# The first batch of a fused attention and feed-forward kernel, worked in two parts of its tokens

## The chip, the core and the metric

The kernel runs on one core of one Trainium2 chip. The metric is device microseconds (us) of one execution, lower is better. All times are of the same inputs, drawn with a fixed seed.

## The reference

Two stages. The first is attention that keeps only the scores within `tau` of the row's maximum; the second takes the largest of three products and multiplies it out again.

```python
q, k, v: (8, 8, 576, 64)        # batch, heads, tokens, head size; float32
scores = q @ k.T / 8
scores = where(scores >= max(scores) - tau, scores, -1e9)     # tau = 0.02, by row
attn = exp(scores - max(scores)); attn = attn / (sum(attn) + 1e-9)
x = (attn @ v), heads side by side: (4608, 512)
h = maximum(maximum(x @ w1, x @ w2), x @ w3)                  # w: (512, 768)
out = h @ w_out                                               # (4608, 512), float32
```

## The kernel before

**Tiling.** The 64 heads are worked in 16 groups of four ("quads", two to a batch). A quad's scores come in nine chunks of 128 rows, each chunk of two "halves" of 128 x 576 (`r` is 0 or 1): 288 halves in all, in the order of the list `steps`. Eight of the nine chunks belong to one half of the quad's head pairs each, the fifth is shared; chunks 0, 1, 5 and 6 hold the first 256 tokens of the batch.

**What each letter does.** The order of all work is written out by hand in the table `ORDER`, one letter for each step, in which a digit names one of four PSUM slots (`bank`, 128 x 1024 floats, two banks each). The wrapper `_Ordered` makes every engine run its instructions in exactly that order. A score half passes through these steps:

- `S` (TensorE): `scores`, into a slot. `m` (VectorE): `maximum`, the row maximum, which also leaves a copy of the scores in a buffer z. `s` (VectorE): `threshold`, a tiny step that some halves need.
- `e` (ScalarE): `exponents`, a first pass over the half. `n` (ScalarE) or `k` (VectorE): `numerators`, the second pass with the row sum. Which of the two is decided by a digit in the table `MASKED`: for 1 and 3 the second pass is on VectorE (`masked`), for 0 and 2 on ScalarE, and then a `0` needs the threshold. For 2 and 3 the first pass reads the slot itself, otherwise z (`direct`).
- `r` (VectorE): the reciprocals of a chunk. `p` (GpSimd): one half of the weights P in bfloat16. `t`: an SP-issued DMA that transposes the chunk's P into `ptq`.

`T` transposes q or k of a quad on TensorE, `a` and `c` copy it out (ScalarE and VectorE), `q` copies q with the partition halves swapped (GpSimd). `O` is a product of `ptq` with v, copied into `xt` by `w` (VectorE) or `x` (ScalarE). `F` and `B` are the two halves of a feed-forward piece. A hidden piece (`hid`) computes 128 columns of one of the three x @ w for all 576 tokens, in two runs of 288 tokens, one to each bank of its slot; its contraction is cut in two halves of 64 rows that run side by side in the array ("row-tiled", `halves`), and `B` swaps the two. The first of the three is copied to a buffer `hm` by ScalarE (`h`), the second is maximised into `hm` and the third into `hT` by VectorE (`v`, `v`). An output piece (`outp`) makes two chunks of 128 rows of the result, copied by `u` and stored by `o`. `N` makes the rows that are left over. `l` issues a load of q, k or v, `g` a load of a block of weights through a double buffer `stage`, `z` casts it on GpSimd, `y` casts v.

**The parts.** `SPLIT` names batches whose tokens are worked in two parts, chunks 0 and 1 first (256 tokens) and then chunks 2 to 4 (320 tokens): the scores, products and feed-forward pieces of the first part come before those of the second. Before, this is the last batch alone (batch 7), so that the program's end does not wait for all of its scores. There a hidden piece has a single run, on all 128 rows of the array, and an output piece is one chunk.

Of the kernel before, what the change touches and what calls it, by code (L numbers as in the profile page):

```python
# [21 lines left out]
FLAT = 2.0 ** -100  # L22

MASKED = """
232222322322222222021032222202332122123122200200111000000000100000000011
000010111020011000101000000001100001001000010011111100000000100100000000
110010030111000100010000000001010100001110001011010100110000000000000000
100101101011000000120000001010000000110011100000001110001000010011111021
"""


# [10 lines left out]
gS0pmelT2mqnS3tcpemqS2nlkT1eytaS0rmnT1kpermS3yS2enczrmS1qT0enmepnqtS3nprmaymgpeS0lptS2mppT0mtpS1enencnqsS3re  # L42
rmtpS0mS1penmS3lqnsS2mtperpekzllmT0tmpenkT1pgS3eearnS0petmnqrS2meqlnpS3lmnplsS2cetpremS1pS0nmplermtzeS3mnS2p
mtnpmS3rkpS1leektS0emnrpmemptS1eekS2pO3mktS0rennmpermT2pnS1wptemS3prkyO0tmeakS2pgS1enxlnrmS0lpesS2mezT3mS1np
mgntspcS2eqrseT3mtpeS0srmapS1mnT2ptS3mnqO0ceqmeO1prswnptnkS3pxS0meF1meS2zBresmT0qghF3klpF2nkBtaS1sveS0pemF3B
nyrrsmyBepT1svS0hpcT2nS3zmaS1erpgsF2mntpsBmnS3yvF1etssT0myeBprS2cnpS3mnS0ympelF2epF3lmBnzslssvS0htBrqmeS2vpn
S1gF0sepmF3teqBmF2erssvpBtnBkphF0eS1vtS3znmF2nrBmqteS1rpvBnS3pmlnF0pmgeS1qsBsrhmS3pevS2npS1mF0npsO3ermpesmO2
zewepgsskBxtT3nF1vS2nklBarS0mlphS3mtepF2sS1rmnyBmetF3pvT0eBpcnS2tzT1nvS0asmzS3temS2qeS1meF0trkpmS3lenpBmnlys
reklpF1umerpskS3upBeoketmS0uS2umpS3tesmS1qeT0myO2nqlrsnlprcO3etqsmepwS0xptS1mnF3psnmS2BlerskpS1thF0meF3pmeBF
2ktnBveBsrS1nvpS0hmyF3emF2npBrssT0eprtvBaF1kS3nqvBeF0myhyS2kyleF3mBelBvnpS2snsS0vptemS1pnF3rmpT2tnBmpeF0scS1  # L50
htBrnmpF3erT2rpvlBasS1pstvnS2pmeF0pS3emtBqnmT2S1hcqS3empF2eS0rsqmtS1epsmBeF3pmnF0stsvBeBknF2klhF1BvelS0nrvpB
emT3pS2arvS0ptnS3mpnO1smtesrkpeF2swnlrpmeT0S1qtescS3epBmnpmnT0trskS3paS1umS0ulqmeS3lmyS1nopS2smelS0rmeS3psmn
O1ypersmqO2etkpemO0lewqxlknpS3tS1keF2momS3lexF0ktT1enkBercpnsBpumN1ertkphkF3jS0rursS1empBnmF2ptS0vpS1smeF3yt
BsnsmBpnvS0pT1hmF2atT3srepS0cF1eprBsmeqF3vnByBynvplS2nsS0plmhS1mteS2mF0nF3mteS1rrspBnmS2pelvBlepF1smT0leqBvl
# [50 lines left out]
def kernel(  # L105
# [31 lines left out]
    NF = DF // 128  # L137
# [341 lines left out]
    def ffn(b, part):  # L479
# [46 lines left out]
        def outp(cs):  # L526
# [16 lines left out]
                my["h"][0]()  # L543

            def done(a):
                if a == 0 and (part is None or c % 2 == 0):
                    st["ob"] = hp_.tile([128, 2, DM], F32, name="ob")
                both = st["ob"]
                ob = both[:, a if part is None else c % 2]
# [6 lines left out]
                if part is not None:  # L556
# [36 lines left out]
        def ninth():  # L593
# [10 lines left out]
            def done():  # L604
# [225 lines left out]
```

## Time and profile before

| | |
|---|---|
| timed runs (3), median | 446.8 us (446.54 to 447.92) |
| the profiled execution: span | 444.8 us |
| TensorE matmul busy | 422.4 us, 95% |
| ScalarE busy | 403.0 us, 91% |
| VectorE busy | 392.8 us, 88% |
| GpSimd busy | 311.9 us, 70% |
| the chain that ended last | 86% TensorE, 5% ScalarE, 4% VectorE |

No time of the profiled execution is given beside its span; the median of the timed runs is 2.0 us above that span. In the profile PE is TensorE, PEld its weight loads, DVE VectorE, ACT ScalarE, POOL GpSimd, SP the engine that issues most DMAs. Nearly every instruction has the line of the helper `run` (L93 before, L95 after), so groups are told apart by the names of what they write and read: sc are scores, tp transposed q and k, o the products, ph hidden pieces, po output pieces, z the score halves on their way (`stage` too, which lends its buffers to them later on).

### The profile page before, as it was taken

How to read it: one execution, taken by the hardware profiler on the slowest of the kernel's cores; microseconds unless marked ns; L12 is line 12 of the kernel's file. 1: busy time of each engine (PE TensorE's matmuls, PEld its weight loads, DVE VectorE, ACT ScalarE, POOL GpSimd, SP SyncE). 2: the span in 40 equal slices, each digit the busy share in tenths (PEclk: the TensorE clock that was granted, in tenths of full speed). 3: DMA queues.
4: the chain of work that ended last, by engine and by line, in shares of the span. 5: the costliest groups of instructions: out<-in, count | busy, mean ns of one | idle time of the engine just before them, and what ended most of it. 6: DMA issues, size and time to landing. Idle time of an engine off the chain costs nothing.

```text
span 444.8 us, 14254 instructions
## 1 busy us (share of the span) xinstructions
PE 422.4 (95%) x5188; PEld 320.2 (72%) x5190; DVE 392.8 (88%) x1228; ACT 403.0 (91%) x836; POOL 311.9 (70%) x420
## 2 busy tenths in 40 slices
PE   7767789999999999999999999999999999999996
PEld 6334347787788767787788777788688886787873
DVE  3887999999999999999999999998999998899642
ACT  3999999999999999999999999899999999987632
POOL 2799989997878687696785877676676685457400
PEclk8998999999999999999999999999999999999999
DMA  7999999999999999699899999989999977487633
GB/s 188 275 293 199 291 169 269 235 243 262 229 180 194 212 222 292 125 256 167 143 234 189 230 198 203 209 168 210 208 206 194 244 151 105 83 179 136 145 116 108
DMA packets 213959, 88.50 MB, mean 199 GB/s; under 512 B 189184, under 2 KB 202240, under 8 KB 213888
## 3 DMA queue, kind: packets, MB, share of 16 engines
q1 hardware_dynamic: 213360, 86.96, 95.9%
q8 instruction: 41, 0.67, 0.6%
q10 hardware_dynamic: 528, 0.62, 0.5%
q14 instruction: 30, 0.25, 0.2%
HBM read 35.65 MB, written 9.44 MB: 101 GB/s over the span
## 4 chain that ended last, share of the span: by engine, by line
PE 86%; ACT 5%; DVE 4%; issue 2%; DMA 1%; SPq 0%; DVEq 0%; ACTq 0%
PE ph L93 32%; PE sc L93 32%; PE po L93 10%; PE o L93 9%; ACT z L93 5%; PE tp L93 3%; DVE z L93 3%; DMA qm<-in_q_dram 1%; ACT qt L93 1%; SPq L93 0%; DVE xt L93 0%; DVE hm L93 0%; DVE stage L93 0%; DVE rs L93 0%; ACT ob L93 0%
## 5 line engine op out<-in xcount | busy, mean ns | idle before, releaser
L93 POOL TENSOR_SCALAR P<-z,rs 128x576 bf16<-128x576 f32 x250 | 200.6, 814 | 63.3 <-DVE rs L93 28.1
L93 DVE TENSOR_SCALAR_CACHE_REDUCE z<-sc 128x576 f32<-128x576 f32 x250 | 183.7, 750 | 14.8 <-PE sc L93 10.1
L93 PE MATMUL sc<-kt,qs 64*128 64x256 f32 (+2 forms) x640 | 182.6, 423 | 5.7 <-DVE z L93 2.3
L93 PE MATMUL sc<-kt,qt 64*128 64x320 f32 (+2 forms) x640 | 182.4, 433 | 5.2 <-ACT z L93 3.3
L93 PE MATMUL ph<-xt,w 64*128 64x288 bf16 (+2 forms) x2160 | 170.8, 283 | 0.1
L93 PEld LDWEIGHTS <-w 64*128 64x128 bf16 (+1 forms) x2160 | 130.1, 94 | 28.6 <-issue 4.3
L93 ACT ACTIVATE z<-z 128x576 f32<-128x576 f32 x174 | 117.6, 679 | 0.1
L93 PEld LDWEIGHTS sc<-kt,qs 64*128 64x128 f32 (+1 forms) x640 | 92.4, 180 | 25.7 <-DVE z L93 5.7
L93 ACT ACTIVATE z<-z,th 128x576 f32<-128x576 f32 x143 | 106.2, 769 | 5.0 <-DVE th L93 4.2
L93 PEld LDWEIGHTS sc<-kt,qt 64*128 64x128 f32 (+1 forms) x640 | 91.9, 179 | 19.7 <-ACT z L93 5.9
L93 DVE SCALAR_TENSOR_TENSOR z<-z 128x576 f32<-128x576 f32 x76 | 62.2, 830 | 0.5 <-ACT z L93 0.5
L93 PE MATMUL po<-wo,hT 64*128 64x512 bf16 (+3 forms) x454 | 53.5, 354 | 0.3
L93 POOL COPY qs<-qt 64x640 f32<-64x640 f32 (+3 forms) x66 | 43.0, 652 | 10.8 <-ACT qt L93 7.2
L93 ACT ACTIVATE z<-z,nm 128x576 f32<-128x576 f32 x68 | 50.6, 767 | 0.0
L93 DVE TENSOR_TENSOR hm<-ph,hm 128x576 bf16<-128x576 f32 (+2 forms) x54 | 37.0, 686 | 9.2 <-PE ph L93 8.9
L93 ACT ACTIVATE hm<-ph 128x576 bf16<-128x576 f32 (+2 forms) x54 | 31.8, 589 | 13.4 <-PE ph L93 12.8
L93 POOL TENSOR_SCALAR P<-stage,rs 128x576 bf16<-128x576 f32 x38 | 30.4, 804 | 19.3 <-ACT z L93 5.4
L93 PEld LDWEIGHTS <-hT 64*128 64x128 bf16 (+2 forms) x456 | 30.0, 95 | 16.5 <-issue 2.3
L93 DVE TENSOR_TENSOR hT<-ph,hm 128x576 bf16<-128x576 f32 (+2 forms) x54 | 37.0, 686 | 4.0 <-PE ph L93 2.3
L93 PE MATMUL o<-ptq,vb 128*64 128x64 bf16 (+2 forms) x544 | 39.0, 281 | 0.0
L93 ACT ACTIVATION_READ_ACCUMULATOR z<-z 128x1 f32 x174 | 34.3, 197 | 0.0
L93 PEld LDWEIGHTS <-vb 128*64 128x64 bf16 x544 | 23.3, 111 | 12.8 <-issue 4.9
(45 smaller groups left out, 431.6 us busy)
## 6 DMA issues: line engine op xcount, KB each, us to landing
vm<-in_v_dram SPq DMA_DIRECT2D x32, 256.0 KB, 4.8
qm<-in_q_dram SPq DMA_DIRECT2D x15, 512.0 KB, 5.0
km<-in_k_dram SPq DMA_DIRECT2D x15, 512.0 KB, 5.3
out_dram<-ob SPq DMA_DIRECT2D x14, 512.0 KB, 4.0
stage<-in_moe_w_dram SPq DMA_DIRECT2D x9, 512.0 KB, 5.2
ptq<-P SPq DMA_TRANSPOSE x144, 4.0
vr<-in_v_dram SPq DMA_DIRECT2D x16, 128.0 KB, 3.4
stage<-in_moe_w_out_dram SPq DMA_DIRECT2D x3, 512.0 KB, 4.9
```

Source lines behind the costliest of these rows:

```text
L93: ins = fn(*a, **kw)
```

## The change

- Batch 0 is put into `SPLIT` too, with the same two parts as batch 7, and into a new set `PAIRED`.
- In a paired batch a hidden piece holds two groups of 128 hidden columns (2f and 2f+1) of one part's tokens, one group to each bank of its slot, instead of one group with two runs of tokens. So it stays row-tiled with two halves `F` and `B`; there are 9 such pieces a part, 18 in the batch as before. Their maxima are kept in `hT` from the first of the three on, with no `hm`.
- Its output pieces are (0, 1) and (2, 3) instead of (0, 2) and (1, 3), one after each part.
- `ORDER` and `MASKED` are written anew. `ORDER` has four `O` more (40 for 36, with two `w` and two `x` more), since batch 0 has eight half-sized products for four. In `MASKED`, 95 halves have their second pass on VectorE (86 before) and 27 their first pass from the slot (41 before).

```diff
-SPLIT = {7: ((0, 1), (2, 3, 4))}
+SPLIT = {0: ((0, 1), (2, 3, 4)), 7: ((0, 1), (2, 3, 4))}
+
+PAIRED = {0}
...
-llllllglllT0laclT1laclzllqqS0qqS1meS2mS3lmlT0enlkS1ylmlT2eamelrnpS3leqlmnyS1qcapS0emtnrcS3pmnT2qmepgrelS1qya
+lllllllllT3lcalqqT1S0lacqqlmS3lemlkegT0lS2calnT1qS3lycamlmqelqreqS2gynpS0nmlpS1ezmreS2lpmpeT0mgyaknT1qT3cT0a
...
-        gap = 2
-        chunks = ([(0, 2), (1, 3)] if part is None else [(c,) for c in mine]) + ([4] if part is None or 4 in part else [])
+        paired = part is not None and b in PAIRED
+        gap = 1 if paired else 2
+        chunks = ([(0, 2), (1, 3)] if part is None else [tuple(mine)] if paired else [(c,) for c in mine]) + \
+            ([4] if part is None or 4 in part else [])
...
-        nr, n = len(runs), runs[0][1] - runs[0][0]
+        nr, n = 2 if paired else len(runs), runs[0][1] - runs[0][0]
...
-                c0, c1 = runs[a]
+                c0, c1 = runs[0 if paired else a]
+                k = 2 * f + a if paired else f
                 return (my["ps"][:, a * 512:a * 512 + n],
-                        lambda rows: wts[wi][rows, kc, f * 128:(f + 1) * 128],
+                        lambda rows: wts[wi][rows, kc, k * 128:(k + 1) * 128],
...
-                    st["hm", f] = hp_.tile([128, nr, n], BF16, name="hm", bufs=3)
+                    st["hm", f] = h_of(b)[:, 2 * f:2 * f + 2, S * (b % 2) + runs[0][0]:S * (b % 2) + runs[0][1]] if paired else hp_.tile([128, nr, n], BF16, name="hm", bufs=3)
...
-                    dst = hm if wi == 1 else \
+                    dst = hm if wi == 1 or paired else \
...
+                if paired:
+                    if a == 1:
+                        stores.append(lambda: sync.dma_start(
+                            out=rows_out[:, 0:8].rearrange("p (x c s) m -> p x s c m", x=2, c=2)[:, :, c // 2], in_=both))
...
-        return ([hid(f, wi) for f in range(NF) for wi in range(3)],
+        return ([hid(f, wi) for f in range(NF // 2 if paired else NF) for wi in range(3)],
...
-                later = [outs.pop()] if part is not None and part != parts_of(b)[-1] else []
+                later = [outs.pop()] if part is not None and b not in PAIRED and part != parts_of(b)[-1] else []
```

Three places in the order. The first is TensorE after its first scores: here stand the transpositions (tp) of the second quad's q and k. Before, they are spread among the scores of the first quad:

```order
131 L93 MATMUL tp<-identf,qm 128x64 x8
132 L93 MATMUL tp<-identf,q_147 128x64 x2
133 L93 MATMUL sc<-kt,qt 64x320 x2
134 L93 MATMUL sc<-kt,qs 64x256 x2
135 L93 MATMUL sc<-kt,qs 128x256
136 L93 MATMUL sc<-kt,qt 128x320
137 L93 MATMUL tp<-identf,km 128x64 x8
138 L93 MATMUL tp<-identf,k_149 128x64 x2
```

After, all four stand together, behind the eighth score half, and the next score is the second quad's:

```order
127 L95 MATMUL sc<-kt,qs 128x320
128 L95 MATMUL sc<-kt,qt 128x256
129 L95 MATMUL tp<-identf,qm 128x64 x8
130 L95 MATMUL tp<-identf,q_147 128x64 x2
131 L95 MATMUL tp<-identf,km 128x64 x8
132 L95 MATMUL tp<-identf,k_149 128x64 x2
133 L95 MATMUL tp<-identf,qm 128x64 x8
134 L95 MATMUL tp<-identf,km 128x64 x8
135 L95 MATMUL sc<-kt,qs 128x256
```

The first quad has eighteen score halves; before, all of them came first.

The second place is SP's queue around the eighth transposed chunk. Before (rows 23, 25 twice, 28 three times and 30 are the second to the eighth; `stage` is a load of weights):

```order
25 L93 DMA_TRANSPOSE ptq<-P 128x9x128 x2
26 L93 DMA stage<-in_moe_w_dram 128x4x256
27 L93 DMA vr<-in_v_dram 64x8x64
28 L93 DMA_TRANSPOSE ptq<-P 128x9x128 x3
29 L93 DMA vr<-in_v_dram 64x8x64
30 L93 DMA_TRANSPOSE ptq<-P 128x9x128
```

After (row 33 is the eighth):

```order
26 L95 DMA stage<-in_moe_w_dram 128x4x256
27 L95 DMA_TRANSPOSE ptq<-P 128x9x128
28 L95 DMA vm<-in_v_dram 64x4x256 x2
29 L95 DMA_TRANSPOSE ptq<-P 128x9x128
30 L95 DMA stage<-in_moe_w_dram 128x4x256
31 L95 DMA_TRANSPOSE ptq<-P 128x9x128
32 L95 DMA stage<-in_moe_w_dram 128x4x256
33 L95 DMA_TRANSPOSE ptq<-P 128x9x128
```

Ahead of the eighth stand seven weight loads after the change, four before.

The third place is VectorE at its first feed-forward maximum, which stands behind 55 row maxima before:

```order
92 L93 SCALAR_TENSOR_TENSOR z,sm<-z 128x576 x2
93 L93 TENSOR_SCALAR th<-nm 128x1
94 L93 TENSOR_TENSOR hm<-ph,hm 128x576
95 L93 TENSOR_SCALAR z,nm<-sc 128x576
96 L93 RECIPROCAL rs<-sm 128x2 x2
```

and behind 34 after, two in a row and of two groups of 256 tokens each:

```order
70 L95 TENSOR_SCALAR th<-nm 128x1
71 L95 RECIPROCAL rs<-sm 128x2
72 L95 TENSOR_TENSOR hT<-ph,hT 128x2x256 x2
73 L95 TENSOR_SCALAR z,nm<-sc 128x576 x2
74 L95 COPY kt<-tp 128x2x256
```

So the first batch's pieces have moved forward past some twenty score halves.

More of the change, by code (lines that the diff above doesn't have):

```diff
@@ L24 @@
 MASKED = """
[L25 to L28, printed above, removed]
+122222122222220303001010100100100000301001203001300200001230000001301020
+000110100001001010100010000100110001011100011100101010000000100010010100
+000100102011110010100010000001001010000011111001101100000100000000000101
+000011110100110000001100000010000000101111000110020110001000110011201003
 """
@@ L45 @@
[L45 to L54, printed above, removed]
@@ new lines @@
+pnS3lmeprsmntpmeS2gpseT0mS1znkS2etyS3esrgkpnmapmO1etzT0wnS2lrmepT1cO3agpsnrmS0lpxsS1lemqO3lekO2pnswrmxS3zeS0
+tmeF1pkF2ngqF3esBmBnqkBhF0qesrsBrvteS1pvS2nlpmF3hzmeT1BcnptS0ssngvF1pS2mepBretmS3zeF2mpnrsvS3pnBtmepS1gepS0s
+rmT3hzmteS1skpF0agmnBS2pevO3tkeyS0rnwmeS3pmnO2ytmpnT1lszxF3celBrskepS1evS2trznmT3S0ntsmpF1alkpelrmS2elpBmeqn
+sktS2eplO3muupS0srwnS2pmeO1mqeT3ktpS2xnrsF1cnT0mqtS3aqrsBlmeyT0phS2sctnS3pmF0eprS1metpBsmnF3pveS2tyBremS0pet
+vynpmF3ekS1qntS0smeT2ByrkapS1nsmlS2hprlmF0epS3mnBtqssmeF1lpvT2elS3psrncBpmeS0tS2psnvlO3nmqleqmO1erwpleskF2px
@@ new lines @@
+S0kntS3mnS1rmBepS0mepS3trmhpnsmS2pteF0srmpeS3skytT2nS1maBrmntyS2pveF3peS1smpBnsmS0tynrvS2pleT1mpS3ectqT0nmF1
+eymtnsrklS2eplsT3amBeylkqelcS0nsrS2spmuO3umqekpS2ewtS0nS1prmnS3pmO2essyrmepmS0elpS1smxS3pnsmtF2qeF0mlBnlrkBp
+hS3srevF2tpeS1mlpS0nmBpnF3myS1evBetkF0elF2mhBorkpS1nssF3vetBysmpeBlrS0evpS1hsmpT2eF3meF0tkBakBnqF2tvnS1srvpn
+S3trmBeplS0smhpS1oempT2lF3nmyS0ncBteF1srmpS2evT0qBmaF3pnlrsvS0peS2smS1pntmBeF0rmphS2keBqF1nmtT3qevBF2pesrvlS
+0epclT1nBpsmS3aktF0nkF1hBsrmepBrveO2ptevpnS3swqS1tnmF2pnrkpteS3meS0pmS1tnrmBpesmpeS0tkuT3essrO1cputekS3yxmoS
@@ new lines @@
+2nmlpT0eS1mqeS3mO2nktaO1rnkpewS0epmS2xsyrsmF3pekyetS1meqS0mnlqBmnlpskleT0N1rucpluskpS2jS3nmtF0erS1rmpeS2mpBm
+F3phS1ssekptT2nBmlT0arvlpS1ecF2lpS3nmqS0estmF1eBomBnvS3htrkS0pnF2lssssemF1yBemBntvyS3pervS0peF2srmpF1emBptnB
+kphF0sreS3vS2pnmBpeF1vnT3qBmaS0slhS2meS3srnS1mtpF0nmpF2esBrmpF3esvpBetBvqF0hkqS1tnS2meBrmT3epO1vnplceT0kF2at
+S3sswnqBmeT0O1rvnpcetqF2xklS0pnrsS1lmnS3ymeBptS0shsyrmS1eF2rmpetF3mBpeS0vpnBsmpteT1S2vpaS0nmtS1nsrmF2pnmtpes
+S3kyeS1mByermpelskS3nqS0emO1tpemlnqrS0wupS3meF1tpkenO0kuktnT2rmlpxBceplrsrS0kpluS3usmoF2eymS1eS0ismpBeS3mpht
@@ new lines @@
+S1nmpF0emS2S3nsrssmpBnF1pveT2trBmaF0veqS3tkeByF1hkF2temBplnS0ssvpoBemlS3erlrS1vpnF0mnqF2tsmeBpBkhF1ynrS3svpn
+S0mtBperS2vepF3mnpT1BmptS0hspF2nmT3BcaS0elsqvS3S1nmF2tersrpmF0nBmpBevqT3hS1scpteF2mplT0nS3klS1asmBeqO0mtesnk
+O1erwpevF3ptxS0skyeS2srF1mnBmetpBvlS0phS2srnmqF1nmT3pF0erctBypeBsvT3yS2pvaS1nmpS3temS0qlnmF2emtnS3rkpleS1rml
+S0epBmepsmpT1uO3cetkelO1kulnkF0yxwosrkepS1teS2mpnS3mBeyrsmpeS2kpuS3tumN1nlmqeorkS2pjlS3emlF1pssT0meS2ketF3rB
+armpBhkpF0nF1trvnBqsBvS3phrsF0tempS1espS2mS3nqBsmetF1pmnF2pvBnS3psevBteysrF0mpF1hkpBntF2ervT3pBncBpvS0hrS3se
@@ new lines @@
+pmT2epS1maS0slmF3nmF2nBsteBrsvpS1eipvT0nF3smqeS2tBmS1lhcF2nsS3mtnBsrspeS0vS1pemO2nqmtemT3lnS0wS1amF2etF3rsmp
+eBspS0nvS1eqmBnF2rkpF0htsmBeS3pveS1rmeO2pmnptknByS3xvS1nrmT2tpS0ssmepS3meyF1cnemS0teS2rmplBnkyermO3pusklepO2
+ulwepkT3xS1akS0leT2smF3nrcptesmS1poeS2rmpeF0lkBeqmnBkqtuS2usslS1hmqS3lnrmpF0eF2kyBesmF1etBrrvpnS3ospBnvF0mhp
+S2etspBmnF3prvS1epBnmT0tpvS2aS1smeqtT3F0ncqS2ermtBpF3khpS1esmBnF0psvtF2emBeBvnS1tkhS3rnmT0pF2asrspmF1eByeqS3
+vS0npsrmF2tepBmnBpsvS3hyS0sremqF2tepS1smS3npmBepmO0ntvesF3keS1rtswpBnsF2mpeF0vnT1BrncpS3htprS1mnBmeT3S2vaS1t
@@ L74 @@
+F0vF3hF1vF2vN0F3juF2uoifod
 """
@@ L545, in done @@
             def done(a):
-                if a == 0 and (part is None or c % 2 == 0):
+                if a == 0 and (part is None or paired or c % 2 == 0):
                     st["ob"] = hp_.tile([128, 2, DM], F32, name="ob")
                 both = st["ob"]
-                ob = both[:, a if part is None else c % 2]
+                ob = both[:, a if part is None or paired else c % 2]
                 src = my["ps"][a]
@@ L555, in done @@
                 scalar.activation(out=ob, in_=src, func=AF.Copy)
-                if part is not None:
+                if paired:
+                    if a == 1:
+                        stores.append(lambda: sync.dma_start(
+                            out=rows_out[:, 0:8].rearrange("p (x c s) m -> p x s c m", x=2, c=2)[:, :, c // 2], in_=both))
+                elif part is not None:
                     stores.append(lambda: sync.dma_start(out=rows_out[:, (0, 2, 1, 3)[c + a]:8:4], in_=ob))
```

28 lines of the change are left out of this document (6 added, 22 removed).

## The prediction

> **What bounds the kernel now.** I read the page first (span, engine shares, the chain), then a table of stretches, then the waits, and last the chain in order of time. The stretches are cut where the order table of the kernel before has its 72nd, 96th, 120th, 144th and last (288th) row maximum; these "marks" are used throughout.
>
> ```profile
> core 0: 444.8 us, clock 0.988
> PE 86%; ACT 5%; DVE 4%; issue 2%; DMA 1%; SPq 0%; DVEq 0%; ACTq 0%
> core 0: us, PE busy (x) PEld busy (x) DVE busy (x) ACT busy (x) POOL busy (x), PEclk, DMA share, GB/s
> 0.00:17.10 17.10, 12.85 (x112) 9.16 (x114) 8.51 (x29) 9.42 (x19) 5.73 (x15) 0.90 0.88 226
> 17.10:97.70 80.60, 68.08 (x735) 45.28 (x729) 73.67 (x231) 79.25 (x172) 74.67 (x98) 0.96 1.13 243
> 97.70:130.50 32.80, 32.80 (x409) 26.20 (x407) 31.28 (x97) 32.59 (x67) 26.29 (x34) 1.00 1.14 233
> 130.50:163.60 33.10, 33.10 (x447) 25.51 (x443) 32.30 (x106) 33.01 (x70) 25.79 (x36) 1.00 1.16 200
> 163.60:199.40 35.80, 35.71 (x484) 27.79 (x482) 33.66 (x111) 34.56 (x70) 27.88 (x37) 1.00 0.99 230
> 199.40:411.90 212.50, 211.39 (x2740) 165.20 (x2738) 199.22 (x630) 201.66 (x415) 146.64 (x198) 1.00 0.95 181
> 411.90:444.80 32.90, 28.48 (x286) 21.06 (x283) 14.21 (x34) 12.53 (x30) 4.87 (x7) 0.99 0.44 125
> 0.00:97.70 97.70, 52.37 (x143) 0.95 1.08 240
> ```
>
> The last row is the same kind of table for VectorE's work on the scores alone (two records a maximum, so 72 by 97.7 us). TensorE is idle 4.3 us in the first stretch, 12.5 in the second, about 1.2 from there to 411.9, and 4.4 at the end. So from the 72nd mark on the kernel is TensorE's, and before it somebody else's: ScalarE is idle only 1.35 us between 17.1 and 97.7. The waits of the first 70 us say the same; TensorE's score matmuls wait for ScalarE's exponentials to free a bank (columns: total, times, longest):
>
> ```profile
> PE sc L93 <- ACT z L93: 4.0, 9, 0.7
> ```
>
> The profiled execution has a span of 444.8 us; the median of the three timed runs is 446.8, 2.0 us more, which I carry over unchanged. About 0.3% (1.3 us) is what a measurement of this kernel can tell from no change.
>
> **The change part by part.** Prices first. For TensorE they come from unbroken pieces of the chain (start, length, line, records):
>
> ```profile
> 154.39 1.36 PE o L93 x20
> 158.48 1.30 PE po L93 x12
> 160.02 4.45 PE sc L93 x35
> 176.95 0.98 PE ph L93 x16
> 412.43 1.37 PE o L93 x30
> 415.15 7.97 PE ph L93 x72
> 423.12 1.53 PE o L93 x40
> 426.05 9.78 PE ph L93 x72
> ```
>
> A score of four records is 0.51; a whole-batch product 1.36; a hidden piece 0.98; an output piece 2 x 1.30. The last batch, split already, prices the split forms: two second-part products 1.53, so 0.77 each; a first-part product 1.37 - 0.77 = 0.60; 18 pieces of 256 tokens 7.97 and of 320 tokens 9.78, so a paired piece (two groups at once) is 0.89 or 1.09. No row shows a paired piece; by columns of the unsplit piece it would be 0.87 and 1.09, so the ends lie 0.02 apart. Nine of each make 17.8 against 18 x 0.98 = 17.6, eight split products 5.5 against four whole ones 5.4: the new form costs TensorE 0.2-0.3 us in all, and has as many evacuations by area. What matters is the place in the order.
>
> VectorE and ScalarE prices are the distances of starts:
>
> ```profile
> 121.15 0.67 ACT L93 ACTIVATE stage<-stage 128x576 f32<-128x576 f32 x1
> 121.81 1.43 ACT L93 ACTIVATE z<-z,nm 128x576 f32<-128x576 f32 x2
> 123.15 0.64 ACT L93 ACTIVATE xt<-o 128x576 bf16<-128x576 f32 x1
> 123.68 0.68 ACT L93 ACTIVATE z<-z 128x576 f32<-128x576 f32 x1
> 119.49 0.15 DVE L93 TENSOR_SCALAR th<-nm 128x1 f32<-128x1 f32 x1
> 119.55 0.75 DVE L93 TENSOR_SCALAR_CACHE_REDUCE z<-sc 128x576 f32<-128x576 f32 x1
> 408.27 0.75 DVE L93 SCALAR_TENSOR_TENSOR z<-z 128x576 f32<-128x576 f32 x1
> 408.95 0.75 DVE L93 SCALAR_TENSOR_TENSOR z<-z 128x576 f32<-128x576 f32 x1
> ```
>
> An exponential pass of either kind is 0.67 on ScalarE (two from 121.81 to 123.15), an evacuation of 576 columns 0.53. On VectorE a masked numerator is 0.68, a threshold 0.06; the maximum of a feed-forward piece, also 576 columns from a bank, I price like these at 0.67.
>
> Now the order up to the 72nd maximum. Before, TensorE has issued 14 hidden pieces and 4 products: 13.7 + 5.4 = 19.1 us. After, it has issued one score more, 9 paired pieces of the first part, 7 of the second, one output piece, 4 + 4 split products and 2 whole ones: 0.5 + 8.0 + 7.6 + 2.6 + 5.5 + 2.7 = 26.9. So it is **7.8 us of TensorE work ahead**. ScalarE has two first passes more (+1.3), three numerators fewer (-2.0), two output copies (+1.0), the extra product evacuations (+0.5) and fewer first passes straight from a bank (+0.6): **+1.4 us**. VectorE has ten thresholds, four masked numerators, two feed-forward maxima and three half evacuations more: 0.6 + 2.7 + 1.3 + 0.5 = **+5.1 us**. Counted alike at the next marks:
>
> | mark | 72 | 96 | 120 | 144 |
> |---|---|---|---|---|
> | before, at us | 97.7 | 130.5 | 163.6 | 199.4 |
> | TensorE work ahead | +7.8 | +2.1 | +3.7 | -1.5 |
> | ScalarE work more | +1.4 | -2.0 | +0.5 | -4.0 |
> | ScalarE idle before, so far | 9.0 | 9.2 | 9.3 | 10.6 |
> | VectorE work more | +5.1 | +3.5 | +5.9 | +3.2 |
> | VectorE idle before, so far | 15.5 | 17.0 | 17.8 | 20.0 |
>
> After the mark, TensorE has the same total to do less what it is ahead. If ScalarE is idle 9.0 us in all after the change (what it idled up to mark 72 before), the gain that TensorE still holds at a mark is "ahead" minus "ScalarE more" plus the ScalarE idle time beyond 9.0: 6.4, 4.3, 3.5, 4.1 us. So most of the 7.8 us is handed back between marks 72 and 120, where the new order asks more of ScalarE and VectorE than of TensorE. I take 4.0, the mean of the last three.
>
> Two things come off. First, the split needs the second four heads ten scores earlier: their four transpositions follow the eighth score, and their k load stands where it stood, behind one weight load.
>
> ```profile
> 9.67 0.74 ACT L93 ACTIVATE z<-sc,nm 128x576 f32<-128x576 f32 x1 [1.32 <-DVE z L93]
> 11.81 0.85 SPq L93 DMA_DIRECT2D km<-in_k_dram  x1
> km<-in_k_dram SPq DMA_DIRECT2D x1, 512.0 KB, 7.0
> 11.00:22.00 11.00, 8.28 (x84) 3.98 (x82) 9.02 (x27) 11.00 (x25) 7.71 (x14) 1.00 1.19 280
> ```
>
> It lands at 18.8 us. Before, ScalarE has other chunks and works 11.00 of 11.00; after, what it has from its first pass (9.67 us) to that point is seven first passes, four numerators and three copies of transposed q, 4.7 + 2.7 + 1.2 = 8.6 us, so about 18.3 us without a wait; then it needs the load and its transposition (0.5), at 19.3: 0.5 to 1.5, I take **1.0**.
>
> Second, the first four products wait for the eighth transposed chunk, which is moved behind a weight load. On SP's queue, shown with the change, the load ahead of it (row 32) must wait until GpSimd has cast the load two before it, a cast that stands behind the 18th half of P. Two halves and a cast (0.81 and 1.04 us) put the eighth up to 2.7 us later than its data.
>
> ```profile
> 39.90 1.41 SPq L93 DMA_TRANSPOSE ptq<-P  x1
> ptq<-P SPq DMA_TRANSPOSE x15, 5.5
> L93 POOL TENSOR_SCALAR P<-z,rs 128x576 bf16<-128x576 f32 x250 | 200.6, 814 | 63.3 <-DVE rs L93 28.1
> L93 POOL CAST w<-stage 128x1024 bf16<-128x1024 f32 x9 | 9.3, 1035 | 7.9 <-DMA stage<-in_moe_w_dram 7.9
> ```
>
> Before, the eighth was issued at 39.9; with 5.5 to land the products could start at 45.4 to 48, and they are wanted at about the 32nd score, some 45 us. Ahead of it SP now issues seven weight loads where it issued four, 1.5 MB more, and the loads for the second batch come later in return; the DMA engines' share is over 1 there already, so a later landing is likelier than an earlier one. Queued behind the products on TensorE are all later scores; ScalarE has two or three passes in hand. Ends: 0 and 3 us; I take **0.7**.
>
> The clock bears on that upper end. Between 33 and 44 us the granted clock was 0.81, after TensorE had stood idle, and the same matmul took 0.63 us there and 0.38 a little later:
>
> ```profile
> 33.00:44.00 11.00, 7.94 (x68) 5.25 (x68) 8.54 (x28) 10.57 (x24) 10.62 (x14) 0.81 1.12 191
> 44.49 0.63 PE L93 MATMUL sc<-kt,qs 64*128 64x256 f32 x1
> 46.54 0.38 PE L93 MATMUL sc<-kt,qs 64*128 64x256 f32 x1
> ```
>
> [...]
>
> So ScalarE allows 4.0 - 1.0 - 0.7 = 2.3 us. VectorE has its own limit. At a mark the gain is "ahead" minus "VectorE more" plus 15 to 20 us of old idle time minus its new idle time: 15.6, 15.6, 15.3 less the new idle time at marks 96, 120, 144. At mark 72 (97.7 + 1.4 + 1.7 = 100.8 us, with 82.2 + 5.1 us worked) that is 13.5 already, which leaves 1.8 if VectorE then never waits until mark 144; before, it waited 4.5 us there. That ScalarE could be kept at 1.35 us of idle in 80 says that a bounding engine can be fed. I allow 0.3: **gain 1.5 us**.
>
> The end of the program has the same pieces in both; the ninth output now precedes the last two in TensorE's order, so that the last copy follows its last matmul: I count nothing there.
>
> **The rivals.** *The lead is kept.* Nine z buffers let the engines run apart, so marks 96 to 120 bind less than I count, and the 6.4 us of mark 72 less 1.7 stay: gain 4.7, 442.1 us. For it: ScalarE is 97 to 100% busy in those stretches already without hurting TensorE. Chance 0.17. *VectorE takes the place (slower).* If it waits 4.5 us between marks 72 and 144 as before, the gain is 15.3 - 13.5 - 4.5 = -2.7: 449.5 us, with TensorE idle for VectorE's maxima at 100 to 200 us. It decides from 1.8 us of waiting on. For it: between marks 72 and 120, 65.9 us before, ScalarE then needs 64.7 (32.59 + 33.01 - 0.9) and VectorE 64.4 (31.28 + 32.30 + 0.8); against it: ScalarE alone was as full before and TensorE did not wait. Chance 0.28. *Nothing comes of it.* The early pieces stand early in the order but start late, behind loads and transposed chunks; the lead at mark 72 is spent on waits, and 0.2 us of longer forms remain: 447.0. Chance 0.15.
>
> **How the numbers follow.** Forecast: 446.8 - 1.5 = 445.3 us, chance 0.40. Its own ends are 2.3 us gained and 0.8 lost (a product wait of 3 for 0.7). The range goes from 441.4, the kept lead (6.4 - 1.0) with no wait for the products, to 449.5. Of the forecast's chance 0.25 lies over 1.3 us faster, 0.13 within, 0.02 slower; the kept lead is all faster; VectorE's case 0.03 within, 0.25 slower; the last 0.11 within, 0.04 slower. So faster 0.42, within 0.27, slower 0.31.
>
> **What would show it.** Right: at the 72nd maximum the span stands at 99.5 to 102 us, TensorE idle 5 us less so far than the old 16.8; first feed-forward matmul near 45 us; ScalarE idle about 1 us near 20 us; VectorE 98% busy from 100 to 200 us. Wrong: over 3 us of TensorE idle after 100 us, a wait of the first products over 3 us, or the 72nd maximum before 98 us.

## The result: 3.4 us slower, and the profile after

The changed kernel takes 450.19 us (median of 5, 448.71 to 451.24) against 446.80 of the kernel before in the same session: ratio 1.0074, 95% interval 1.0053 to 1.0095. The forecast was 445.3 us, range 441.4 to 449.5. The profiled execution has a span of 448.4 us and took 450.19, 1.8 more. The medians differ by 3.4 us and the two profiled spans by 3.6; what follows divides the 3.6.

First the page of the kernel after, its core line and its chain by engine, which was 86% TensorE before:

```profile
core 0: 448.4 us, clock 0.990
PE 68%; DVE 11%; issue 6%; DMA 6%; POOL 4%; ACT 3%; SPq 1%; DVEq 0%; POOLq 0%; ACTq 0%
```

VectorE, the transposed chunks and GpSimd have come onto the path. Next, the stretches of both kernels, cut where a comparison is exact: at 123.10 us before and 124.88 us after, TensorE has the same pieces left. The columns are as in the prediction's table (the kernel before first, then after):

```profile
0.00:123.10 123.10, 106.33 (x1152) 74.08 (x1152) 106.59 (x334) 113.90 (x240) 101.73 (x139) 0.96 1.11 240
123.10:436.00 312.90, 311.65 (x4010) 244.08 (x4013) 285.08 (x894) 287.53 (x594) 210.14 (x282) 1.00 0.94 184
436.04:444.80 8.76, 4.40 (x29) 2.05 (x27) 1.13 (x2) 1.58 (x3) 0.00 (x0) 0.98 0.40 138
```

```profile
0.00:124.90 124.90, 106.99 (x1192) 75.47 (x1194) 109.10 (x347) 111.81 (x233) 105.10 (x142) 0.97 1.09 244
124.90:439.80 314.90, 313.34 (x4010) 238.01 (x4011) 292.47 (x906) 287.23 (x585) 213.64 (x279) 1.00 0.92 181
439.81:448.40 8.59, 4.50 (x29) 1.97 (x27) 1.13 (x2) 1.47 (x3) 0.00 (x0) 0.89 0.30 107
```

That gives the loss in two parts (TensorE has 4010 records in the second row of each). The first batch, the head of the program, costs **1.8 us**: TensorE is idle 17.9 instead of 16.8 us, and busy 0.7 longer. The rest takes **2.0 us** longer, of which 1.7 is busy time and 0.3 idle. The last 9 us give 0.2 back. No lead is left at 123 us: it is a lag already. TensorE's 1.1 us of added idle time in the first batch are 0.6 up to the 32nd maximum, 0.9 less from there to the 72nd, and 1.4 behind it, where it was never idle before.

Where the lead was to be won, up to the 72nd maximum, VectorE's work on scores and the stretches of all engines after the change (the last row is the prediction's own cut, 72 maxima, now at 104.2 us):

```profile
0.00:48.50 48.50, 35.00 (x322) 23.63 (x322) 36.33 (x115) 37.93 (x79) 35.78 (x54) 0.93 1.06 255
48.50:66.60 18.10, 16.53 (x213) 12.10 (x213) 16.61 (x53) 18.00 (x38) 15.99 (x20) 1.00 1.20 251
48.50:104.20 55.70, 52.71 (x661) 38.69 (x660) 53.17 (x168) 53.86 (x113) 50.00 (x63) 1.00 1.10 241
104.20:124.90 20.70, 19.28 (x212) 13.14 (x212) 19.60 (x68) 20.02 (x42) 19.33 (x27) 1.00 1.13 226
0.00:104.21 104.21, 52.73 (x143) 0.97 1.08 247
```

The 32nd maximum stands at 48.5 us after and 48.4 before. From there to the 72nd the four engines are busy 90 to 97% of 55.7 us, where the kernel before needed 49.3. The pieces were moved forward, and the scores moved back by nearly as much. No single engine makes up the chain over that stretch:

```profile
by line: DVE z L95 18.6%; DMA ptq<-P 18.1%; ACT z L95 15.8%; issue 14.0%; PE sc L95 8.4%; POOL P L95 7.0%; PE o L95 4.9%; SPq L95 3.1%; DVE hT L95 2.6%; ACT xt L95 1.9%; DVE kt L95 1.8%; PE ph L95 1.3%; DVE th L95 1.1%; ACT hT L95 1.1%; DVE
```

The chain of the kernel after over 36 to 68 us (start, length, line) shows the first products and what they wait for; the timeline below it, the first feed-forward matmul:

```profile
41.17 0.53 SPq L95
41.70 0.05 issue
41.75 5.52 DMA ptq<-P
47.27 0.04 issue
47.31 1.25 PE o L95 x19
48.57 0.79 PE sc L95 x4
```

```profile
49.61 0.82 PE L95 MATMUL ph<-xt,w 64*128 64x256 bf16 x12
```

The eighth chunk is issued at 41.75, behind the weight load at 41.17, and lands 5.5 us later.

### The profile page after: what moved, and what is told of

It reads as the page before. It is cut to its first block, busy times and chain, and to the rows that moved or that the text cites. A ratio compares the mean times of both kernels' runs of the same rounds, so it can differ in the third digit from the quotient of the medians.

```text
span 448.4 us, 14357 instructions
## 1 busy us (share of the span) xinstructions
PE 424.8 (95%) x5228; PEld 315.4 (70%) x5230; DVE 402.7 (90%) x1253; ACT 400.5 (89%) x820; POOL 318.7 (71%) x420
## 4 chain that ended last, share of the span: by engine, by line
PE 68%; DVE 11%; issue 6%; DMA 6%; POOL 4%; ACT 3%; SPq 1%; DVEq 0%; POOLq 0%; ACTq 0%
PE ph L95 26%; PE sc L95 23%; DVE z L95 8%; PE po L95 8%; PE o L95 8%; DMA ptq<-P 6%; PE tp L95 3%; POOL P L95 2%; ACT z L95 2%; POOL qs L95 1%; PE warm L95 1%; DVE stage L95 1%; DVE hT L95 1%; POOL vb L95 1%; SPq L95 1%
## 5 line engine op out<-in xcount | busy, mean ns | idle before, releaser
L95 PE MATMUL sc<-kt,qs 64*128 64x320 f32 (+2 forms) x640 | 176.6, 415 | 7.5 <-POOL qs L95 4.1
L95 PE MATMUL sc<-kt,qt 64*128 64x256 f32 (+2 forms) x640 | 177.7, 426 | 3.2 <-DVE z L95 2.5
L95 PE MATMUL ph<-xt,w 64*128 64x288 bf16 (+4 forms) x2160 | 166.8, 283 | 1.2 <-DVE hT L95 0.6
L95 PEld LDWEIGHTS <-w 64*128 64x128 bf16 (+1 forms) x2160 | 126.0, 94 | 33.6 <-issue 8.3
L95 ACT ACTIVATE z<-z,th 128x576 f32<-128x576 f32 x148 | 110.6, 768 | 3.0 <-DVE th L95 2.2
L95 ACT ACTIVATE z<-z 128x576 f32<-128x576 f32 x167 | 112.7, 677 | 0.3
L95 DVE SCALAR_TENSOR_TENSOR z<-z 128x576 f32<-128x576 f32 x83 | 72.1, 876 | 0.0
L95 ACT ACTIVATE z<-z,nm 128x576 f32<-128x576 f32 x75 | 56.7, 768 | 1.2 <-DVE z L95 1.2
L95 DVE TENSOR_TENSOR hm<-ph,hm 128x576 bf16<-128x576 f32 (+2 forms) x48 | 32.5, 677 | 9.1 <-PE ph L95 8.7
L95 PEld LDWEIGHTS <-hT 64*128 64x128 bf16 (+2 forms) x456 | 26.6, 95 | 19.6 <-issue 2.7
L95 DVE TENSOR_TENSOR hT<-ph,hm 128x576 bf16<-128x576 f32 (+2 forms) x48 | 32.5, 678 | 2.1 <-PE ph L95 0.2
```

The source lines that it names most:

```text
L95: ins = fn(*a, **kw)
```

## The experiments

Row maxima are counted in each trace. The three kernels with "old" and "new" in their names join the two orders, old_scalar_cut is the kernel before with one edit, and all others are the changed kernel with one edit or, under "Several at once", with several. "Ratio" is to the kernel before, run on the same chip.

| run | us | ratio (95%) | 32nd max | 72nd max |
|---|---|---|---|---|
| before | 446.8 to 447.3 | 1 | 48.4 | 97.7 |
| after | 450.2 | 1.0074 (1.0053 to 1.0095) | 48.5 | 104.2 |
| oldhead_newrest | 453.1 | 1.0135 (1.0114 to 1.0156) | 48.5 | 98.0 |
| newhead_oldrest | 451.3 | 1.0091 (1.0072 to 1.0109) | 48.0 | 104.0 |
| old_to_170_then_new | 451.5 | 1.0097 (1.0074 to 1.0119) | 48.5 | 97.9 |
| const_products | 451.8 | 1.0106 (1.0082 to 1.0130) | 48.2 | 104.4 |
| small_casts | 457.5 | 1.0229 (1.0207 to 1.0252) | 54.8 | 110.3 |
| no_casts | 450.5 | 1.0084 (1.0059 to 1.0108) | 48.8 | 105.2 |
| vector_cut | 450.8 | 1.0091 (1.0071 to 1.0111) | 48.0 | 104.7 |
| scalar_cut | 451.1 | 1.0097 (1.0066 to 1.0127) | 48.6 | 104.8 |
| vector_scalar_cut | 451.4 | 1.0105 (1.0054 to 1.0156) | 48.5 | 102.7 |
| less_matmul | 452.2 | 1.0098 (1.0062 to 1.0133) | 49.0 | 103.9 |
| scalar_cut_early | 450.4 | 1.0066 (1.0038 to 1.0095) | 47.4 | 103.2 |
| swaps_first | 453.3 | 1.0118 (1.0088 to 1.0147) | 50.2 | 106.1 |
| triple_cut | 450.1 | 1.0078 (1.0055 to 1.0100) | 47.4 | 104.2 |
| quadruple_cut | 452.2 | 1.0125 (1.0085 to 1.0165) | 47.5 | 104.5 |
| no_vector_numerators | 451.9 | 1.0112 (1.0091 to 1.0132) | 48.4 | 104.1 |
| all_cut_no_numerators | 451.6 | 1.0117 (1.0084 to 1.0149) | 47.3 | 104.0 |
| nine_moved | 454.4 | 1.0167 (1.0138 to 1.0196) | 48.6 | 105.8 |
| old_scalar_cut | 447.0 | 0.9998 (0.9981 to 1.0014) | 49.1 | 98.4 |

**Head or rest.** Two kernels join the orders at the 104th maximum, one at the 170th. (The edits here and below are abridged.)

```
SPLIT = {7: ...}; PAIRED = set()   # or SPLIT, PAIRED as after
MASKED, ORDER: one kernel's up to the row maximum, then the other's
```

> The first batch unsplit and in the old order up to the 104th row maximum, from there the new order and flags. Head theory (the split's early waits cost the time): as before, 446.3 to 447.3. Rest theory (full VectorE and ScalarE after mark 72 hand a lead back): no lead here, so as before too, or up to 0.5 less. End theory (what the new order does after mark 104, its last 36 us above all, costs the time): 449 to 450.

> The first batch split and paired and in the new order up to the 104th row maximum, from there the old order and flags. Head theory: 449.5 to 450.5, as after. Rest theory: the lead is partly kept, 445 to 447. End theory: 447.0 to 448.0, that is before plus the 1.0 us by which the 104th maximum stands later in the trace.

> The first batch unsplit, old order and flags up to the 170th row maximum, from there the new order and flags; at that maximum the two orders stand at nearly the same work, so the joint should cost little. Theory that the rest of the new order costs time by itself: in the traces TensorE of the changed kernel falls back another 1.2 us from there to the end at equal work, so 447.5 to 448.8. Theory that all of the loss comes from the first batch: 446.3 to 447.3.

All three came out slower than any theory said, because the joints cost time themselves: TensorE is idle for 3.6, 2.0 and 3.1 us within 25 us behind them, so their ends decide nothing. Their stretches do. Between two places with equal work left (some 192 and 413 us before), in the order before, after, oldhead_newrest, newhead_oldrest:

```profile
191.52:413.09 221.57, 220.44 (x2856) 172.71 (x2856) 207.71 (x657) 210.57 (x432) 154.88 (x209) 1.00 0.95 184
```

```profile
194.03:416.81 222.78, 221.54 (x2856) 166.81 (x2856) 211.86 (x661) 212.08 (x429) 159.30 (x208) 1.00 0.91 178
```

```profile
196.36:418.88 222.52, 221.32 (x2857) 167.02 (x2856) 211.68 (x661) 211.95 (x429) 158.76 (x208) 1.00 0.92 179
```

```profile
195.65:417.64 221.99, 220.78 (x2856) 172.95 (x2856) 207.88 (x657) 210.56 (x431) 153.97 (x209) 1.00 0.95 183
```

With the same number of matmuls the new order takes 1.2 and 0.9 us longer in the two kernels that have it, and the old one 0.4 in the one that got it later; nearly all is TensorE's busy time, not waits. The ends of these stretches differ by four matmuls, of products in the one order and of output pieces in the other. Cut where nothing differs (190.26 to 412.36 us before, 192.77 to 416.10 after), it is 1.2 us too, 1.1 of them busy. Nor is it noise of one trace: where two kernels have the same order, as old_to_170_then_new and the kernel before up to 230 us, every score from 100 to 230 us starts 0.23 to 0.25 us later in the one than in the other. So the rest costs something by itself, whatever the head. The head's part is confirmed too: newhead_oldrest is 1.7 us late at the place that the kernel before passes at 123.1 us, and the old rest gives none of it back.

**The waits for chunks and the casts.**

```
const_products:  pt[...] -> vrs[2] (zeros)  if L["b"] == 0 else pt[...]
small_casts:     pool.tensor_copy(out=dst[:, 0:1, 0:64], ...); vector.memset(w, 0.01) at the start
no_casts:        pool.tensor_copy(out=few, in_=my["t"][:, 0:64]); one constant weight tile
```

> The changed kernel, but the products of the first batch read a constant tile of zeros instead of the transposed chunks, so none of the eight waits for a transposition (the first batch's output is wrong by that). Theory of the chunk waits: the first four products run at 40 to 43 us, the first feed-forward matmul at 43 to 46, the 72nd maximum at 101 or before, the end 2.5 to 4 us earlier than after, 446.2 to 447.7. Theory that ScalarE, VectorE and GpSimd are full anyway: first feed-forward matmul earlier all the same, but the 72nd maximum within 1 us of 104.2 and the end within 1 us of 450.2.

> The changed kernel, but each of the twelve weight casts on GpSimd converts 64 columns of one block instead of 1024, the rest of the weights being a constant set at the start on VectorE (the output is wrong by that). It takes some 11 us off GpSimd before mark 72. Theory that the casts, five more of them before 62 us than before the change, keep the halves of P and so the transposed chunks late: the seventh and eighth transpositions issue 3 us earlier, first feed-forward matmul at 46 or before, 72nd maximum at 101 or before, end 447.5 or less. Rival (GpSimd has room, ScalarE sets the pace): all within 1 us of the changed kernel, 449.5 to 450.7.

> The changed kernel, but the twelve weight casts on GpSimd write 64 columns of a tile that nobody reads, and the four weight tiles are one constant, set on VectorE before the first transposition comes (output wrong by that): the start is not delayed this time, 1 us or so is off GpSimd for each cast, and no feed-forward matmul waits for a weight. Theory that GpSimd, full from 17 to 61 us, keeps the head back: 32nd maximum at 46.5 or before, 72nd at 101 or before, end 447.5 or less. Rival, VectorE or ScalarE does: 72nd within 1 us of 104.2, end within 1 us of 450.2.

const_products: the first feed-forward matmul at 49.3 us (49.6 after), the 72nd maximum where it was. The products stand so late for their place in TensorE's order, not for the chunks alone. small_casts is no test: the four memsets held VectorE until 14.5 us, and the 8th maximum came 9.6 us late; no_casts, without that delay, moved nothing. Neither was what held the head.

**One engine at a time.**

```
few = 64 if <masked / not masked / any> and 32 <= half < 96 else S ; z = z[:, 0:few]
scalar_cut_early: not masked and 4 <= half < 32
less_matmul:      for kc in range(3 if paired else 4)
swaps_first:      ...T0mgaknT1qT3cT0aqceqS1nqyzmn...   (y, z behind the four q)
old_scalar_cut:   the cut of scalar_cut in the kernel before
```

> The changed kernel, but the 19 masked numerators of halves 32 to 95 work on 64 of their 576 columns (output wrong by that): some 0.6 us each, 11 us in all off VectorE between about 45 and 130 us; their thresholds stay. Theory that VectorE sets the pace there (it is idle 0.7 us from 72.6 to 113.0 us after the change): the 72nd maximum at 101 or before, the 96th at 131 or before, the end 3 us or more before the changed kernel's, 447.2 or less. Theory that ScalarE does: all within 1 us of the changed kernel (104.2, 134.1, 450.2). If both are about equally full: 1 to 2.5 us earlier.

> The changed kernel, but the 45 second passes of ScalarE for halves 32 to 95 work on 64 of their 576 columns (output wrong by that): some 0.55 us each, 25 us in all off ScalarE between about 45 and 130 us. Theory that ScalarE sets the pace there: 72nd maximum at 100 or before, the end 447.2 or less. Theory that VectorE does: all within 1 us of the changed kernel. If both are about equally full: 1 to 2.5 us earlier.

> The changed kernel, but the 18 paired pieces of the first batch add three of the four blocks of x instead of four (output wrong by that): a quarter of 9 x 0.89 + 9 x 1.09, 4.4 us of TensorE work less, 3.9 of it before the 72nd maximum; nothing else changes. Theory that TensorE itself sets the pace from 48 us on (cutting VectorE or ScalarE there moved nothing): 72nd maximum at 100 to 101, the end 4 to 4.5 us before the changed kernel's, 445.7 to 446.3. Theory that another engine sets the pace of the first batch: 72nd maximum at 103.5 to 104.5; the end then 449 or more if the lead is handed back later, 446 if it is kept.

> The changed kernel with both cuts at once: all 64 numerators of halves 32 to 95, on VectorE and on ScalarE, work on 64 columns (output wrong by that), 11 us off the one and 25 off the other. Theory that TensorE sets the pace from 48 us on: 72nd maximum at 103.2 to 105.2, end 449.5 to 451.3, as with either cut alone. Rival, the two are full together, so that one cut only hands the bound to the other: 72nd maximum at 100 or before, end 447.2 or less.

> The changed kernel, but the 20 second passes of ScalarE among halves 4 to 31 work on 64 columns (output wrong by that): 11 us off ScalarE between 12 and 48 us. Theory that ScalarE sets the pace up to the 32nd maximum, as it is idle 3.1 us from 16.7 to 48.5: 32nd maximum at 45 or before, the end 2 us or more earlier than the changed kernel's, 448.2 or less. Rival, the loads, the transposed q and GpSimd set it: 32nd maximum within 1 us of 48.5, end 449.5 to 451.3.

> The changed kernel with the four swapped copies of q that the tenth score waits for moved on GpSimd ahead of one weight cast and one cast of v (1.7 us): nothing is left out. My term of 1.0 us for the start: the first scores of the second quad come 1 to 1.7 us earlier, 16th maximum at 28 or before, and the end about 1 us earlier, 449.0 to 449.5. Rival, what is gained there is waited for later (the second weight load now waits for the cast): 32nd maximum within 0.4 us of 48.5, end 449.8 to 451.

> The kernel before, its 46 second passes of ScalarE for halves 32 to 95 on 64 of 576 columns (output wrong by that), 25 us off ScalarE: the same cut that moved nothing after the change. The prediction's reading, ScalarE alone sets the pace of the first batch before the change (idle 0.2 us from 48 to 98 us): 72nd maximum at 94 or before (97.7 before), the TensorE idle of 16.8 us down to 13 or less, end 3 us or more earlier, 443.8 or less. Rival, it is full together with others there too: 72nd maximum within 1.2 us of 97.7, end within 1 us of 447.

No cut moved the 72nd maximum by more than 1.5 us, and no median lies below the spread of the changed kernel (448.7 to 451.2). From 48.5 to 104.2 us VectorE was busy 6.9 us less in vector_cut, ScalarE 9.8 in scalar_cut, TensorE 1.9 in less_matmul, and nobody used that slack; "TensorE sets the pace from 48 us on" fell with less_matmul (0.3 us of 3.9). It shows how a lead is lost, too: its scores start 0.7 us ahead of the changed kernel's from 124 to 160 us and up to 0.2 behind from 170 to 320. swaps_first had its 16th maximum 2.0 us earlier (26.8 us), all lost by the 24th, and its 32nd 1.8 later: a load on SP's queue waits 7.0 us for the weight cast that was put behind the swaps and is issued at 22.3 us instead of 17.1, with all that stands behind it. The 1.0 us I had taken off for the start was no price that an earlier start would refund.

The sharpest is old_scalar_cut. Its stretches, and those of the kernel before over the same times:

```profile
48.40:66.60 18.20, 14.28 (x132) 7.16 (x129) 18.08 (x57) 15.15 (x39) 15.32 (x19) 1.00 1.12 216
66.60:97.70 31.10, 30.69 (x410) 24.42 (x412) 30.43 (x98) 25.32 (x68) 29.61 (x40) 1.00 1.13 239
```

```profile
48.40:66.60 18.20, 14.64 (x132) 7.45 (x132) 18.13 (x57) 17.95 (x38) 15.54 (x19) 1.00 1.14 217
66.60:97.70 31.10, 30.74 (x416) 24.58 (x417) 30.31 (x101) 31.10 (x68) 29.49 (x40) 1.00 1.11 250
```

ScalarE's 31.10 of 31.10 looked like the bound; with 25.32 nothing moves. TensorE's 30.74 is the bound there, as the chain of the kernel before over 66.6 to 97.7 us says by itself:

```profile
by line: PE ph L93 44.6%; PE sc L93 40.0%; PE o L93 8.3%; PE tp L93 4.7%; ACT z L93 2.4%; issue 2.3%
```

Over 48.4 to 66.6 us the cut left ScalarE busy 15.15 us instead of 17.95 and moved nothing either. The largest part of the chain there, before the change, is VectorE's, which was busy 18.13 of 18.20 us:

```profile
by line: DVE z L93 45.2%; issue 25.1%; PE sc L93 12.5%; ACT z L93 11.7%; DVE xt L93 2.8%; DVE rs L93 1.9%; DVE th L93 0.9%; DVEq L93 0.1%; ACTq L93 0.1%
```

**Several at once.** triple_cut joins const_products and vector_scalar_cut; quadruple_cut adds less_matmul. The last three take VectorE's masked numerators away or move them:

```
no_vector_numerators: the 19 masked halves of 32..95: digit 1 -> 0, 3 -> 2, k -> n, s added; 64 columns
all_cut_no_numerators: quadruple_cut with these digits and letters
nine_moved: nine halves, digit 1 -> 0, k -> n, s added; 576 columns
```

> The changed kernel with the constant products of the first batch and both cuts of numerators (halves 32 to 95) at once: no wait for a transposed chunk of the first batch, 11 us off VectorE, 25 off ScalarE (output wrong by that). Theory that several are full together, the chunks' round trip among them, so that each cut alone only hands the bound on: 72nd maximum at 101.5 or before, where each cut alone left it at 103.9 to 104.8. Theory that TensorE alone sets the pace: 72nd maximum within 1 us of 104.2.

> The same, and the paired pieces of the first batch with three of four blocks of x, 4.4 us of TensorE work less (output wrong by that). Theory that several are full together: each of the five has slack now, 72nd maximum at 98 or before, 3 us or more ahead of the triple cut. Theory that none of these sets the pace (GpSimd or the loads do): within 1 us of the triple cut.

> The changed kernel, but the 19 masked numerators of halves 32 to 95 go to ScalarE (flags and order letters changed) and take 64 of 576 columns there (output wrong by that): VectorE has no operation on two SBUF operands there, ScalarE some 2.5 us more. Theory of the blocked numerators (in the cuts a 64-column numerator still took 0.2 to 3.2 us, as long as GpSimd's instructions ran on beside it, so the cut did not free VectorE): 72nd maximum at 102.5 or before, end 448.5 or less. Rival (the waits between the engines in this order hold it, whatever one of them has to do): 72nd maximum within 1.2 us of 104.2, end 449 to 451.5.

> The quadruple cut, but all 64 numerators of halves 32 to 95 on ScalarE with 64 columns, none on VectorE (output wrong by that). Theory of the blocked numerators: the 3.2 us stall of the quadruple cut at 68 us goes, 72nd maximum at 99 or before (104.5 there). Rival: 72nd maximum at 102 or later.

> The changed kernel with nothing left out; the nine masked numerators that took over 1.0 us between 17 and 106 us (halves 6, 15, 20, 24, 27, 30, 47, 48, 56) are moved from VectorE to ScalarE: 10.7 us off VectorE, 6.0 onto ScalarE. Theory of the blocked numerators: 72nd maximum at 103 or before, end 448.5 to 449.5. Rival: ScalarE is as full as VectorE, so 72nd maximum at 104 to 107, end 450 to 453.

Triple and quadruple cut did not move the 72nd maximum either. Both traces have a stall of their own, a numerator cut to 64 columns that ran 3.19 us while GpSimd worked beside it (the quadruple's: VectorE's timeline, then GpSimd's):

```profile
68.10 3.19 DVE L95 SCALAR_TENSOR_TENSOR z<-z 128x64 f32<-128x64 f32 x1
```

```profile
67.76 1.03 POOL L95 CAST wo<-stage 128x1024 bf16<-128x1024 f32 x1
68.77 0.74 POOL L95 TENSOR_SCALAR P<-z,rs 128x576 bf16<-128x576 f32 x1
69.46 1.03 POOL L95 CAST wo<-stage 128x1024 bf16<-128x1024 f32 x1
70.47 0.74 POOL L95 TENSOR_SCALAR P<-z,rs 128x576 bf16<-128x576 f32 x1
```

In all_cut_no_numerators that stall is gone, and the 48th, 56th and 64th maxima come 2.9, 1.7 and 2.7 us earlier than after (69.7, 82.8, 91.2 for 72.6, 84.5, 93.9). By the 72nd it is lost again. no_vector_numerators is no clean test of VectorE alone: with the moved numerators ScalarE was busy 55.70 of the 55.70 us. The chain of all_cut_no_numerators names two places of waiting, and its row over 48.5 to 104.2 us shows what the engines had left over:

```profile
75.21 4.71 DMA qm<-in_q_dram
...
93.20 4.48 DMA ptq<-P
```

```profile
48.50:104.20 55.70, 48.82 (x591) 33.71 (x587) 45.55 (x151) 45.78 (x133) 45.16 (x63) 1.00 1.15 242
```

TensorE stands for the q of the fourth quad (54 halves, three quads, are behind it there), loaded only when SP's queue comes to it, and for a transposed chunk. Every engine is idle 6.9 to 10.5 us of the stretch, yet it is no shorter than without the cuts (56.7 us from the 32nd maximum to the 72nd, 55.7 after). So after the change the load of no one of the four engines sets the first batch. What does set it is not shown. One candidate is the hand-overs in the written order: score to maximum to bank, halves to chunk to product, load to transposition. The other is the DMA transfers, and no run took any of those away. The share of the DMA engines is 1.10 in this stretch after the change, 1.15 in the row above and 1.14 and 1.11 in the two rows of the kernel before. From the 32nd maximum to the 72nd they moved 13.4 MB at 241 GB/s after and 11.7 MB at 238 GB/s before, so that the time grew nearly as the bytes did. It is no more than a candidate: before the change a share of 1.14 did not hold up TensorE from 97.7 to 130.5 us, where it was never idle. A run with fewer loads in this stretch would tell the two apart. nine_moved, which leaves nothing out, is slower than after: ScalarE then is the full one, idle 1.3 us from 16 to 72 maxima (3.0 after).

No version beat the kernel before, and none of the runs points to one: the old head with the old rest is the fastest of the four pairings, though two of the other three carry a joint.

## Why the prediction was wrong, step by step

By the spans the forecast was 5.1 us off, 1.5 gained against 3.6 lost. Of that 3.3 us had gone wrong by 123 us (1.5 gained against 1.8 lost), 2.0 are the rest of the order, and the end gave 0.2 back.

- **"From the 72nd mark on the kernel is TensorE's, and before it somebody else's": the step that failed.** From it I took ScalarE as the bound, and its work and idle time as the measure of TensorE's gain. I read TensorE's idle time in one stretch of 80 us and ScalarE's 1.35 us beside it. Cut finer, before the change TensorE is idle 12.9 us up to the 32nd maximum, 3.6 from there to 66.6 us, and 0.4 from there to 97.7. old_scalar_cut shows that ScalarE was the bound in neither of the last two; from 66.6 us on it is TensorE. After the change the first product ran at 42.0 us. Before, TensorE was idle 0.6 us from there to the 32nd maximum, so early pieces could fill at most 0.6 + 3.6 + 0.4 = 4.6 us. I credited 7.8 us of "work ahead", 6.4 of it as a gain at the 72nd maximum. What came was 0.3 there, and 1.8 us lost by 123 us. Why the first batch waits after the change stays open between hand-overs and transfers.
- **ScalarE's formula.** It had ScalarE idle 9.0 us in all and then 1.7 more. By the 32nd maximum it was 1.7 more (10.5 for 8.8), as many as the terms 1.0 and 0.7 together; by the 72nd 3.4 more (12.4), and its work was 3.1 more where I counted 1.4 (a first-pass total of 46.4 for 44.0 us, and one feed-forward copy that I missed). So that mark came at 97.7 + 3.1 + 3.4 = 104.2, not 100.8. The gain there, TensorE's idle 16.8 less 16.5, is 0.3 where I had 4.7.
- **The wait of the first products**, taken as 0.7 with ends 0 and 3, was 1.2 for the eighth chunk, and the three waits for chunks between 40 and 105 us make 2.2. In range; but const_products shows that it bought nothing to take them away.
- **The split's own cost**, 0.2 to 0.3, is not shown by itself. TensorE was busy 0.7 us longer up to 123 us at equal work, but at another mean clock (0.97 for 0.96).
- **VectorE**, priced 5.1 us dearer, was busy 7.3 longer: its numerators took 0.90, not 0.68, in the head (0.85 before). It then waited 2.5 us from the 72nd to the 144th maximum, where I allowed 0.3. The slower rival's number (449.5) was near, its sign right; its mechanism did not show: VectorE relieved by 6.9 us in vector_cut moved nothing.
- **What I counted at nothing**: that the rest of the program, ordered anew, would take as long. It takes 2.0 us more at equal work. The end itself, counted at nothing too, gave 0.2 back.
- **The clock.** It had no term in the forecast, only a bearing on a long wait of the products. That wait was 1.2 us; the granted clock was 0.93 up to 48.5 us and 1.00 from there to 439.8 us, so the paired pieces ran at 1.00. A wait inside my range could have cost more than its length: in triple_cut a stretch at 0.50 came behind an idle time of 2.5 us (last section). That is an estimate of mine; no run shows it for the products.

Of the signs that I named, two came near: VectorE 97.6% busy from 100 to 200 us (forecast 98), and ScalarE idle 0.8 us from 17 to 22 us (about 1). The rest did not: the 72nd maximum at 104.2 us (99.5 to 102), the first piece at 49.6 (45), TensorE's idle time hardly changed there. A late 72nd maximum was not among my signs of being wrong.

## What to carry to other kernels

Work moved earlier is worth no more than the idle time of the bounding engine in the places that it can reach; cut the windows until each has one bound, and find where the bound changes hands, before counting a lead. An engine at 100% in a window need not be the bound there when another stands at 99% (ScalarE 31.10 and TensorE 30.74 of 31.10 us before the change): the chain over that window, or one run with the engine relieved, tells. Count the DMA transfers among the things that may bind (18.1% of the chain over 48.5 to 104.2 us after the change): I relieved every compute engine and never them. And compare two orders where they have equal work left, so that a lead, a wait and a longer way through the same work show apart.

## What the runs showed of the hardware

A VectorE numerator cut to 64 columns took 0.21 to 0.22 us with GpSimd idle (quadruple_cut, four cases from 126 us on) and 3.19 beside four GpSimd instructions in a row, ending 0.1 us after the last (rows above). It did not always last to the end of such a row: in vector_cut a numerator at 62.2 us took 0.51 and ended 0.1 us after the first of two GpSimd instructions. What makes it longer is not shown.

TensorE's granted clock was 0.50 in some stretches that lie in or behind idle times. In the kernel after it was 0.50 from 19.8 to 26.6 us, and no gap between two of TensorE's matmuls up to there was over 2.1 us. In triple_cut TensorE was idle 2.5 us from 69.3 us, and the clock was 0.50 from 73.05 to 76.45, where an output piece took 2.23 us instead of 1.30 (the two rows of windows, after and triple_cut, then the piece):

```profile
19.80:26.60 6.80, 5.77 (x22) 4.00 (x24) 3.95 (x13) 4.77 (x12) 6.55 (x10) 0.50 1.19 249
73.05:76.45 3.40, 3.40 (x19) 2.30 (x16) 1.58 (x8) 2.14 (x5) 2.55 (x4) 0.50 0.90 178
72.84 2.23 PE po L95 x12
```

The mean of 0.81 in the prediction and that of 0.93 after the change come from such stretches; in the kernel before, the clock was 0.50 from 31.5 to 34.8 us, behind gaps of at most 1.43, and from 41.65 to 45.04 us, where the prediction's matmul of 0.63 us stands. What brings the clock down is not shown.

2856 matmul records take TensorE 220.4 to 220.8 us in the old order and 221.3 to 221.5 in the new one, at full clock with hardly a gap. So the order of the same work alone is worth some 0.2 to 0.5 per cent here. What in the order does it was not tried.
